# The add of 1e-9 under the softmax, on six columns written in pairs in place of four to four

## The chip, the cores and the metric

The kernel runs on one core of one Trainium2 chip. The metric is the device time of one execution in microseconds (us); of several runs the median is given. TensorE is called PE in the profile, VectorE DVE, ScalarE ACT, GpSimd POOL and SyncE SP; PEld is TensorE's loading of weights.

## The reference

Sliding-window attention with a distance bias, and behind it a feed-forward layer with a squared Relu, all in float32:

```python
# q, k, v: (8, 8, 576, 64): batch, heads, positions, head size
scores = scale * np.matmul(q, k.transpose(0, 1, 3, 2))
bias = slopes[:, None, None] * (-np.abs(rel))          # rel = query position - key position
mask = (rel >= 0) & (rel < 128)
scores = np.where(mask, scores + bias, -1e9)
scores = scores - np.max(scores, axis=-1, keepdims=True)
attn = np.exp(scores)
attn = attn / (np.sum(attn, axis=-1, keepdims=True) + 1e-09)
out = np.matmul(attn, v)
# heads side by side: x is (4608, 512); w_in (512, 2048), w_out (2048, 512)
h = np.maximum(x @ w_in, 0.0)
return h * h @ w_out
```

The change is at the 1e-09 and the division by the sum.

## The kernel before

The 4608 rows are cut into 9 chunks of 512, and each chunk has 4 pairs of heads. A *segment* is half a chunk for one pair of heads: 256 queries and two heads, as four blocks (`m` = 0 to 3) of 128 queries, two blocks to a head. There are 72 segments, and each runs through the same steps:

- *scores* on PE into PSUM;
- `top(m)`, four times on DVE: adds the distance table, writes the sums to the tile `t` (negated and scaled) and their minimum over the row, which is the negated maximum of the scores, to a column of the small tile `nm`;
- `exp(m)`, four times on ACT: the exponential with that column as bias, and the row's sum into another column of `nm`;
- `sums()`, on DVE: the add of 1e-9 to the four sums (L264) and the reciprocal (L265), both into a third group of columns of `nm`;
- `norm()`: the multiplication of `t` by the four factors, on POOL (L268, and L608 in the wide segments of the start), for segment 7 on DVE with one instruction for each block (L606);
- a transposition, the matmul with the values, and the split of the result `X` into a high and a low part `xu` (L307 and L310 in the start).

The feed-forward layer multiplies in float32 by splitting each operand into two parts and taking three matmuls of 128x512 for each tile. `gemm1` (L200) makes 128 rows of `h` from the four `xu` of a chunk; Relu (L210), square and the split into `hh` and `hl` (L219) follow; `gemm2` (L229) adds up the output over the 16 blocks of 128 rows. The weights arrive packed, 16 blocks of two DMAs (L165), and each block is converted in five steps: L171 (ACT), L173 and L175 (DVE), L177 (ACT, or POOL for blocks 0, 2 and 15), L179 (DVE).

The *start* covers the first chunk's attention in eight segments of their own kind (`Wide`: the scores of 128 queries against 256 keys, less where there are no earlier keys), the conversion of the weights, and the first chunk's feed-forward. Its transposes are done on PE (L615 for the own keys, L618 for the earlier ones) and copied out by ACT or DVE (L283, L622); L297 is the matmul with the values, L579 that of the scores, L127 matmuls on zeros that keep PE at work. A planner with fixed costs and due times decides the order of the steps on every engine of the start, and this order is kept: the costs that it uses are numbers in the code (0.4 us for `sums`) and do not change with the instructions. Each engine works off its list in order.

From the second chunk on, PE's order is written out by hand, with the attention of coming chunks between the matmuls of the feed-forward, and the scheduler of the framework orders the instructions of the other engines by a timeline of its own. There the norm's result is transposed in blocks on DVE (L319), goes through DRAM and back, and is masked on POOL (L332).

`nm` is one tile for each segment, from a pool of six. Its columns are: 0 to 3 the negated maxima, 4 to 7 the sums, 8 to 11 the sums plus 1e-9 and then their reciprocals. Both instructions of `sums` take four neighbouring float32 columns to four neighbouring ones.

Of the kernel before, what the change touches and what calls it, by code (L numbers as in the profile page):

```python
# [9 lines left out]
F32 = mybir.dt.float32  # L10
# [3 lines left out]
AF = mybir.ActivationFunctionType  # L14
ALU = mybir.AluOpType
# [46 lines left out]
class Kern:  # L62
# [68 lines left out]
    def room(self, c, p, name, shape, offset):  # L131
        if (c, p) != (0, NP - 1):
            return self.ld.tile(shape, F32, name=name)
        at = self.arena + (NF - 1) * 8192 + offset
        return self.nc.alloc_sbuf_tensor_at(f"{name}_", shape, F32, offset=at).ap()
# [103 lines left out]
class Segment:  # L239
# [9 lines left out]
    def top(self, m):  # L249
        self.nc.vector.tensor_tensor_reduce(  # L250
            self.t[:, m], self.t[:, m], self.K.nrel(2 * self.p + m // 2), -0.125, BIG,
            ALU.add, ALU.min, self.nm[:, m : m + 1],
        )

    def exp(self, m):
        nm = self.nm
        return self.nc.scalar.activation(  # L257
            self.t[:, m], self.t[:, m], AF.Exp, bias=nm[:, m : m + 1], scale=-1.0,
            accum_out=nm[:, 4 + m : 5 + m],
        )  # L260

    def sums(self):
        rec = self.nm[:, 8:12]
        self.nc.vector.tensor_scalar(rec, self.nm[:, 4:8], 1e-9, None, op0=ALU.add)  # L264
        self.nc.vector.reciprocal(rec, rec)  # L265

    def norm(self):
        self.nc.gpsimd.tensor_tensor(  # L268
            self.t, self.t, self.nm[:, 8:12].unsqueeze(2).to_broadcast([128, 4, 128]), op=ALU.mult
        )  # L270

    def turn(self):
# [98 lines left out]
class Couple:  # L371
# [113 lines left out]

    def room(self, s):
        K, G = self.K, self.both[s]
        G.t, G.nm = K.tp.tile([128, 4, 128], F32, name="t"), K.sm.tile([128, 12], F32, name="nm")

    def begin(self, s):  # L490
        self.room(s)
# [67 lines left out]
class Wide(Segment):  # L559
# [7 lines left out]
    def scores(self):  # L567
        K, nc, sg = self.K, self.nc, self.sg
        qk = K.qk[self.c, self.p]
        if self.k % 2:  # L570
            self.s = [b.rearrange("p (i c) -> p i c", i=2) for b in K.start_banks[0:2]]
        else:
            s = K.sc.tile([128, 4, 256], F32, name="s")
            self.s = [s[:, 0:2], s[:, 2:4]]
        for i in range(2):
            a, q0, k0 = self.first[i], 64 * (4 * sg + 2 * i) + (0 if sg == 0 else 640), 256 + 128 * (2 * sg + i)
            for j in range(2):
                r = slice(64 * j, 64 * j + 64)
                nc.tensor.matmul(  # L579
                    self.s[j][:, i, a:256], qk[r, q0 : q0 + 128], qk[r, k0 + a : k0 + 256], start=True, stop=True,  # L580
                    skip_group_check=True,
                )
        self.t = K.room_t[self.k % 4]
        self.nm = K.sm.tile([128, 12], F32, name="nm")

    def top(self, m):
        j, i = divmod(m, 2)
        a = self.first[i]
        self.nc.vector.tensor_tensor_reduce(
            self.t[:, m, a:256], self.s[j][:, i, a:256], self.K.wide[self.p][:, j, a:256], -0.125, BIG,  # L590
            ALU.add, ALU.min, self.nm[:, m : m + 1],
        )

    def exp(self, m):
        nm, t = self.nm, self.t[:, m, self.first[m % 2] : 256]
        self.nc.scalar.activation(
            t, t, AF.Exp, bias=nm[:, m : m + 1], scale=-1.0, accum_out=nm[:, 4 + m : 5 + m],
        )

    def norm(self):  # L600
        for i in (0, 1) if self.skip else (None,):
            m, a = (slice(None), 0) if i is None else (slice(i, 4, 2), self.first[i])
            t, rec = self.t[:, m, a:256], self.nm[:, 8:12][:, m]
            if self.k in NORMS:
                for j in range(t.shape[1]):
                    self.nc.vector.tensor_scalar(t[:, j], t[:, j], rec[:, j : j + 1], None, op0=ALU.mult)  # L606
                continue
            self.nc.gpsimd.tensor_tensor(t, t, rec.unsqueeze(2).to_broadcast(list(t.shape)), op=ALU.mult)  # L608

    def turn(self):  # L610
        self.place()
# [273 lines left out]
```

## Time and profile before

| | |
|---|---|
| median of 3 runs | 941.42 us (941.16 to 941.61) |
| profiled execution | 941.43 us, of which the span from first to last instruction is 939.7 us |
| PE busy | 930.5 us (99% of the span) |
| DVE, ACT, POOL busy | 501.4, 416.8, 210.6 us |
| granted clock of TensorE | 1.000 |
| L264, the add | 72 times, 139 ns at the least, 170 in the median, 1042 at the most |
| L265, the reciprocal | 72 times, 177, 178, 182 ns |

The page's own lines give, for each group of instructions, the line, the engine and operation, output <- input with shape and type, the count, the busy time, the mean of one, and the idle time of the engine just before them with what ended it. A row of the timeline gives start and duration in us; neighbouring instructions of the same kind stand in one row, with their count. PE's ends are modelled, since its matmuls overlap.

### The profile page before, as it was taken

Reading aid. Unit: us, or ns where it says so; the run is one execution under the profiler, and the core shown is the slowest. Engines: PE = TensorE matmul, PEld = TensorE weight load, DVE = VectorE, ACT = ScalarE, POOL = GpSimd, SP = SyncE. Lnnn points to the kernel's source line nnn. Section 1 sums busy time; section 2 is a strip of 40 time slices with the busy share of each in tenths; the row PEclk is TensorE's granted clock in tenths of the full one; section 3 lists DMA queues with packets and bytes.
Section 4 is the critical chain, followed back from the end, with each engine's and each line's share of the span. In section 5 each row is a group of like instructions: output and inputs, shape, how many; then the busy total and the mean of one; then the engine's idle time right before and its main releaser. Section 6 shows DMA issues by size and latency. Waiting matters only on the chain.

```text
span 939.7 us, 19487 instructions
## 1 busy us (share of the span) xinstructions
PE 930.5 (99%) x7488; PEld 783.0 (83%) x7492; DVE 501.4 (53%) x1334; ACT 416.8 (44%) x1107; POOL 210.6 (22%) x254
## 2 busy tenths in 40 slices
PE   9899999999999999999999999999999999999998
PEld 5688888888888888888888888888888888888886
DVE  6998874445554554545554444555455454433222
ACT  7898753343444444344433343344444444322222
POOL 4223331222222222222212222221222222220000
PEclk9999999999999999999999999999999999999999
DMA  9975423222432233232433232334322231111001
GB/s 345 404 282 167 134 74 116 73 71 85 129 86 84 76 99 112 67 85 76 128 85 84 69 110 83 85 85 115 101 75 85 74 94 42 39 46 45 1 0 45
DMA packets 72893, 95.26 MB, mean 101 GB/s; under 512 B 8032, under 2 KB 41952, under 8 KB 72800
## 3 DMA queue, kind: packets, MB, share of 16 engines
q1 hardware_dynamic: 72368, 93.36, 32.4%
q8 instruction: 59, 0.97, 0.4%
q10 hardware_dynamic: 432, 0.66, 0.2%
q14 instruction: 34, 0.28, 0.1%
HBM read 67.76 MB, written 26.21 MB: 100 GB/s over the span
## 4 chain that ended last, share of the span: by engine, by line
PE 94%; DMA 4%; ACT 1%; DVE 0%; issue 0%; SPq 0%; ACTq 0%; POOLq 0%
PE acc L229 43%; PE g L200 42%; PE s L539 5%; PE g L546 2%; DMA raw<-in_dram 2%; DMA cst<-in_dram 2%; PE s L546 1%; PE at L344 1%; DMA wide<-in_dram 1%; PE s L410 0%; PE at L410 0%; ACT t L468 0%; ACT raw L171 0%; DVE t L480 0%; ACT t L257 0%
## 5 line engine op out<-in xcount | busy, mean ns | idle before, releaser
L200 PE MATMUL g<-xu,w 128*128 128x512 f32 x1728 | 423.6, 394 | 1.3 <-issue 0.8
L200 PEld LDWEIGHTS g<-xu,w 128*128 128x128 f32 x1728 | 344.2, 209 | 57.1 <-issue 1.7
L229 PE MATMUL acc<-hh,w 128*128 128x512 f32 x1152 | 385.8, 396 | 0.0
L229 PEld LDWEIGHTS acc<-hh,w 128*128 128x128 f32 x1152 | 223.9, 194 | 46.0 <-issue 5.3
L210 ACT ACTIVATE r<-g 128x512 f32<-128x512 f32 x144 | 86.2, 598 | 352.5 <-PE g L200 352.4
L213 DVE TENSOR_TENSOR r<-r 128x512 f32<-128x512 f32 x129 | 93.1, 721 | 256.3 <-ACT r L210 256.3
L229 PE MATMUL acc<-hl,w 128*128 128x512 f32 x576 | 226.4, 393 | 0.0
L332 POOL TENSOR_SCALAR_AFFINE_SELECT pp<-pp 128x512 f32<-128x512 f32 x128 | 111.2, 869 | 219.4 <-DMA pp<-way 156.5
L219 DVE TENSOR_TENSOR hl<-r,hh 128x512 fp32r<-128x512 f32 x144 | 119.3, 829 | 74.8 <-ACT hh L217 72.7
L268 POOL TENSOR_TENSOR t<-t,nm 128x512 f32<-128x512 f32 x64 | 73.8, 1154 | 262.1 <-DVE nm L265 234.9
L229 PEld LDWEIGHTS acc<-hl,w 128*128 128x128 f32 x576 | 112.1, 195 | 19.8
L217 ACT CAST hh<-r 128x512 fp32r<-128x512 f32 x144 | 89.2, 619 | 78.6 <-DVE r L213 77.0
L257 ACT ACTIVATE t<-t,nm 128x128 f32<-128x128 f32 x256 | 100.0, 393 | 12.2 <-DVE nm L250 12.1
L319 DVE STREAM_TRANSPOSE pp<-t 128x512 f32<-128x512 f32 x64 | 45.1, 707 | 44.3 <-POOL t L268 37.6
L250 DVE CUSTOM_DVE_ANT_0 t<-t,cst 128x128 f32<-128x128 f32 x256 | 59.5, 295 | 1.0
L539 PE MATMUL s<-pp,v 64*64 64x128 f32 (+1 forms) x1792 | 52.0, 248 | 0.1
L539 PEld LDWEIGHTS s<-pp,v 64*64 64x64 f32 x1792 | 40.5, 134 | 10.2 <-issue 9.8
L257 ACT ACTIVATION_READ_ACCUMULATOR t<-t,nm 128x1 f32 x256 | 48.2, 188 | 0.0
L480 DVE COPY_PREDICATED t<-cst,s 64x256 f32<-64x256 int32 x100 | 44.6, 446 | 6.7 <-ACT t L461 3.6
L470 POOL MEMSET t<- 64x128 f32 (+1 forms) x44 | 10.0, 229 | 118.4 <-PE s L546 109.4
L527 ACT CAST xu<-s 128x512 fp32r<-128x512 f32 x28 | 16.4, 587 | 41.8 <-DVE t L480 26.8
L468 ACT COPY t<-g 64x256 f32<-64x256 f32 (+2 forms) x86 | 28.0, 340 | 3.8 <-PE g L546 1.0
(68 smaller groups left out, 483.2 us busy)
## 6 DMA issues: line engine op xcount, KB each, us to landing
raw<-in_dram SPq DMA_DIRECT2D x32, 512.0 KB, 8.7
way<-pp SPq DMA_DIRECT2D x256, 64.0 KB, 2.0
pp<-way SPq DMA_DIRECT2D x64, 256.0 KB, 2.7
qk<-in_dram SPq DMA_DIRECT2D x32, 320.0 KB, 3.1
v<-in_dram SPq DMA_DIRECT2D x32, 320.0 KB, 3.9
qk<-in_dram SPq DMA_DIRECT2D x38, 256.0 KB, 4.5
out_dram<-o SPq DMA_DIRECT2D x35, 256.0 KB, 2.7
v<-in_dram SPq DMA_DIRECT2D x3, 256.0 KB, 4.9
```

What stands on the lines that cost most here:

```text
L200: nc.tensor.matmul(g, w, xs[cc][:, part], start=i == 0, stop=i == 11)
L210: self.relu = nc.scalar.activation(r, g, AF.Relu)
L213: nc.vector.tensor_tensor(r, r, r, op=ALU.mult)
L217: nc.scalar.copy(hh, r)
L219: nc.vector.tensor_tensor(hl, r, hh.bitcast(F32), op=ALU.subtract)
L229: nc.tensor.matmul(self.acc[m], w, h, start=(f == 0 and i == 0), stop=(f == NF - 1 and i == 2))
L250: self.nc.vector.tensor_tensor_reduce(self.t[:, m], self.t[:, m], self.K.nrel(2 * self.p + m // 2), -0.125, BIG, ALU.add, ALU.min, self.nm ...
L257: return self.nc.scalar.activation(self.t[:, m], self.t[:, m], AF.Exp, bias=nm[:, m : m + 1], scale=-1.0, accum_out=nm[:, 4 + m : 5 + m],)
L268: self.nc.gpsimd.tensor_tensor(self.t, self.t, self.nm[:, 8:12].unsqueeze(2).to_broadcast([128, 4, 128]), op=ALU.mult)
L319: nc.vector.transpose(squares.rearrange("p b m c -> p m b c"), self.t.rearrange("p m (b c) -> p m b c", c=32))
L332: nc.gpsimd.affine_select(to, self.own, pattern=[[-32 * sign, 4], [0, 4], [-sign, 32]], compare_op=op, fill=0.0, base=0, channel_multiplie ...
L539: made.append(mm(to, w, x, start=first and n < 2, stop=not first, skip_group_check=True))
```

## The change

`nm` has 20 columns. The sums move to columns 0 to 3 and the maxima to 4 to 7. The add reads columns 0 to 5 as one row, the four sums and the first two maxima, and writes them in three pairs that begin at columns 8, 12 and 16. The reciprocal works in place on the first two pairs, so that the four factors lie in columns 8, 9, 12 and 13; the third pair is not used. The norms take the factors from there, as two heads by two blocks.

```diff
     def sums(self):
-        rec = self.nm[:, 8:12]
-        self.nc.vector.tensor_scalar(rec, self.nm[:, 4:8], 1e-9, None, op0=ALU.add)
-        self.nc.vector.reciprocal(rec, rec)
+        pairs = lambda a, n, step: self.nm[:, a : a + n * step].rearrange("p (n c) -> p n c", c=step)[:, :, 0:2]
+        self.nc.vector.tensor_scalar(pairs(8, 3, 4), pairs(0, 3, 2), 1e-9, None, op0=ALU.add)
+        self.nc.vector.reciprocal(pairs(8, 2, 4), pairs(8, 2, 4))
+        self.rec = pairs(8, 2, 4)

     def norm(self):
         self.nc.gpsimd.tensor_tensor(
-            self.t, self.t, self.nm[:, 8:12].unsqueeze(2).to_broadcast([128, 4, 128]), op=ALU.mult
+            *(x.rearrange("p (j i) c -> p j i c", j=2) for x in (self.t, self.t)),
+            self.rec.unsqueeze(3).to_broadcast([128, 2, 2, 128]), op=ALU.mult
         )
```

In `top` and `exp`, of both kinds of segment, the columns change to `nm[:, 4 + m : 5 + m]` for the maximum and `nm[:, m : m + 1]` for the sum. The norm of the wide segments follows:

```diff
-            m, a = (slice(None), 0) if i is None else (slice(i, 4, 2), self.first[i])
-            t, rec = self.t[:, m, a:256], self.nm[:, 8:12][:, m]
+            m, a = (slice(0, 2), 0) if i is None else (slice(i, i + 1), self.first[i])
+            t, rec = self.t.rearrange("p (j i) c -> p j i c", j=2)[:, :, m, a:256], self.rec[:, :, m]
             if self.k in NORMS:
-                for j in range(t.shape[1]):
-                    self.nc.vector.tensor_scalar(t[:, j], t[:, j], rec[:, j : j + 1], None, op0=ALU.mult)
+                for x in range(4):
+                    j, e = divmod(x, 2)
+                    self.nc.vector.tensor_scalar(t[:, j, e], t[:, j, e], rec[:, j, e : e + 1], None, op0=ALU.mult)
                 continue
-            self.nc.gpsimd.tensor_tensor(t, t, rec.unsqueeze(2).to_broadcast(list(t.shape)), op=ALU.mult)
+            self.nc.gpsimd.tensor_tensor(t, t, rec.unsqueeze(3).to_broadcast(list(t.shape)), op=ALU.mult)
```

More of the change, by code (lines that the diff above doesn't have):

```diff
@@ L251, in top @@
             self.t[:, m], self.t[:, m], self.K.nrel(2 * self.p + m // 2), -0.125, BIG,
-            ALU.add, ALU.min, self.nm[:, m : m + 1],
+            ALU.add, ALU.min, self.nm[:, 4 + m : 5 + m],
         )
@@ L257, in exp @@
         return self.nc.scalar.activation(
-            self.t[:, m], self.t[:, m], AF.Exp, bias=nm[:, m : m + 1], scale=-1.0,
-            accum_out=nm[:, 4 + m : 5 + m],
+            self.t[:, m], self.t[:, m], AF.Exp, bias=nm[:, 4 + m : 5 + m], scale=-1.0,
+            accum_out=nm[:, m : m + 1],
         )
     def sums(self):
-        rec = self.nm[:, 8:12]
-        self.nc.vector.tensor_scalar(rec, self.nm[:, 4:8], 1e-9, None, op0=ALU.add)
-        self.nc.vector.reciprocal(rec, rec)
+        pairs = lambda a, n, step: self.nm[:, a : a + n * step].rearrange("p (n c) -> p n c", c=step)[:, :, 0:2]
+        self.nc.vector.tensor_scalar(pairs(8, 3, 4), pairs(0, 3, 2), 1e-9, None, op0=ALU.add)
+        self.nc.vector.reciprocal(pairs(8, 2, 4), pairs(8, 2, 4))
+        self.rec = pairs(8, 2, 4)
     def norm(self):
         self.nc.gpsimd.tensor_tensor(
-            self.t, self.t, self.nm[:, 8:12].unsqueeze(2).to_broadcast([128, 4, 128]), op=ALU.mult
+            *(x.rearrange("p (j i) c -> p j i c", j=2) for x in (self.t, self.t)),
+            self.rec.unsqueeze(3).to_broadcast([128, 2, 2, 128]), op=ALU.mult
         )
@@ L487, in room @@
         K, G = self.K, self.both[s]
-        G.t, G.nm = K.tp.tile([128, 4, 128], F32, name="t"), K.sm.tile([128, 12], F32, name="nm")
+        G.t, G.nm = K.tp.tile([128, 4, 128], F32, name="t"), K.sm.tile([128, 20], F32, name="nm")
     def begin(self, s):
@@ L583, in scores @@
         self.t = K.room_t[self.k % 4]
-        self.nm = K.sm.tile([128, 12], F32, name="nm")
+        self.nm = K.sm.tile([128, 20], F32, name="nm")
     def top(self, m):
@@ L590, in top @@
             self.t[:, m, a:256], self.s[j][:, i, a:256], self.K.wide[self.p][:, j, a:256], -0.125, BIG,
-            ALU.add, ALU.min, self.nm[:, m : m + 1],
+            ALU.add, ALU.min, self.nm[:, 4 + m : 5 + m],
         )
@@ L596, in exp @@
         self.nc.scalar.activation(
-            t, t, AF.Exp, bias=nm[:, m : m + 1], scale=-1.0, accum_out=nm[:, 4 + m : 5 + m],
+            t, t, AF.Exp, bias=nm[:, 4 + m : 5 + m], scale=-1.0, accum_out=nm[:, m : m + 1],
         )
```

## The prediction

> **What bounds the kernel now.** I read the head of the page first, then the busy time of each engine in two stretches.
>
> ```profile
> span 939.7 us, 19487 instructions
> ## 1 busy us (share of the span) xinstructions
> PE 930.5 (99%) x7488; PEld 783.0 (83%) x7492; DVE 501.4 (53%) x1334; ACT 416.8 (44%) x1107; POOL 210.6 (22%) x254
> ```
>
> ```profile
> 0.00:48.00 48.00, 43.19 (x391) 28.85 (x396) 38.44 (x137) 37.35 (x109) 14.99 (x19) 1.00 0.99 375
> 48.00:939.70 891.70, 887.27 (x7098) 754.14 (x7097) 462.93 (x1198) 379.45 (x999) 195.64 (x235) 1.00 0.30 87
> ```
>
> The columns are the stretch, its length, then PE, PEld, DVE, ACT, POOL busy, granted clock, DMA share, GB/s. From 48 us on TensorE is busy 887.27 of 891.70 us and DVE only 462.93: there the add of 1e-9 cannot matter, except by making TensorE wait. What can move the end is how soon the dense stream of matmuls begins. So I read the start, in the groups of DVE work up to 52 us, then in time order.
>
> ```profile
> L264 DVE TENSOR_SCALAR nm<-nm 128x4 f32<-128x4 f32 x9 | 3.6, 405 | 0.2
> ...
> L622 DVE COPY pp<-acc 128x256 f32<-128x256 f32 x4 | 1.7, 414 | 0.2 <-PE acc L618 0.2
> ...
> L606 DVE TENSOR_SCALAR tw<-tw,nm 128x256 f32<-128x256 f32 x4 | 1.1, 350 | 0.0
> ```
>
> ```profile
> 27.55 0.68 DVE L622 COPY pp<-acc 128x512 f32<-128x512 f32 x1
> 28.15 1.21 DVE L175 SCALAR_TENSOR_TENSOR raw<-raw 128x1024 int32<-128x1024 int32 x1
> 29.28 0.41 DVE L310 TENSOR_TENSOR xu<-acc,xu 128x256 fp32r<-128x256 f32 x1
> 29.61 1.04 DVE L264 TENSOR_SCALAR nm<-nm 128x4 f32<-128x4 f32 x1
> 30.69 0.18 DVE L265 RECIPROCAL nm<-nm 128x4 f32<-128x4 f32 x1
> 30.91 1.14 DVE L606 TENSOR_SCALAR tw<-tw,nm 128x256 f32<-128x256 f32 x4
> 31.96 0.42 DVE L622 COPY pp<-acc 128x256 f32<-128x256 f32 x1
> 32.30 1.22 DVE L179 TENSOR_TENSOR w<-raw,w 128x1024 fp32r<-128x1024 f32 x1
> 33.43 0.42 DVE L310 TENSOR_TENSOR xu<-acc,xu 128x256 fp32r<-128x256 f32 x1
> ```
>
> An add of four columns has a mean of 405 ns in the start, and one of them takes 1.04 us in the middle of a stretch in which DVE has no idle time. What it waited for shows in POOL's rows of the same time, beside the add one pair earlier:
>
> ```profile
> 24.12 0.62 DVE L264 TENSOR_SCALAR nm<-nm 128x4 f32<-128x4 f32 x1
> ```
>
> ```profile
> 22.82 1.90 POOL L608 TENSOR_TENSOR tw<-tw,nm 128x1024 f32<-128x1024 f32 x1 [1.37 <-DVE nm L265]
> 25.12 1.61 POOL L608 TENSOR_TENSOR tw<-tw,nm 128x256 f32<-128x256 f32 x2 [0.41 <-DVE nm L265]
> 29.48 1.15 POOL L177 CAST w<-raw 128x1024 fp32r<-128x1024 f32 x1 [2.75 <-ACT tw L596]
> ```
>
> The add at 24.12 ends at 24.74, POOL's norm at 24.72. The add at 29.61 ends at 30.65, POOL's cast at 30.63. Both adds end where POOL ends: they start and are then held until POOL is through. Not every DVE instruction is held so:
>
> ```profile
> 73.30 0.18 DVE L265 RECIPROCAL nm<-nm 128x4 f32<-128x4 f32 x1
> ```
>
> ```profile
> 73.22 0.73 POOL L332 TENSOR_SCALAR_AFFINE_SELECT pp<-pp 128x512 f32<-128x512 f32 x1 [8.53 <-DMA pp<-way]
> ```
>
> Here a reciprocal of the same four columns runs its ordinary 0.18 us in the middle of a POOL instruction.
>
> **The change part by part.** *The add.* 72 adds stay 72, with six columns in place of four, two of them wasted. Whether the new form is held as the old one is shown by no row. One end is that it is: 1.04 us again. The other is the free duration. I get that from the rows before: nine adds take 3.6 us, of which two are 1.04 and 0.62; an add behind nothing I take at 0.17 us, as its neighbour of equal size, the reciprocal, takes 0.18. I take 0.17, since the reciprocal is the nearest one-input row on the same tile and is not held. Two more columns cost nothing I can see: L622 takes 414 ns for 256 columns, under 2 ns a column.
>
> [...]
>
> *The reciprocal* now reads and writes two pairs; four columns still, 0.18 us, 0 either way. *Top and exp* swap their columns only: 0. The add now also reads two maxima, which DVE itself wrote well before the exponentials it waits for anyway: 0. *The larger tile*, 20 columns for 12: 0. *The norm* on POOL reads its factors in two levels in place of one:
>
> ```profile
> L608 POOL TENSOR_TENSOR tw<-tw,nm 128x1024 f32<-128x1024 f32 x3 | 5.7, 1896 | 1.8 <-DVE nm L265 1.4 <-ACT tw L596 0.4
> L608 POOL TENSOR_TENSOR tw<-tw,nm 128x512 f32<-128x512 f32 x4 | 4.2, 1042 | 0.0
> ```
>
> 1024 elements in four rows take 1896 ns, 512 in two 1042: 1.67 ns an element and some 0.19 us fixed, with no sign of a price for a row. I take 0; the bound is in the rivals.
>
> *What the path gets.* First term, the adds before 27.5 us. The one at 24.12 alone gives DVE 0.62 - 0.17 = 0.45 us. But the copy L622 at 27.55 reads what TensorE transposes:
>
> ```profile
> 26.10 0.60 PE L615 MATMUL at<-cst,tw 128*128 128x128 f32 x4
> 26.53 0.60 PE L618 MATMUL acc<-cst,tw 128*128 128x128 f32 x4
> ```
>
> L618 ends at 27.13, and with a hand-over of 0.05 us (the reciprocal at 30.69 starts 0.04 after the add ends) the copy cannot start before 27.18. TensorE runs its own list without a gap there, so it does not come earlier: at most 27.55 - 27.18 = 0.37 us is kept, whatever the earlier adds give. I take 0.37; the lower end is 0.
>
> Second term, the add at 29.61. The cast on POOL waits for L175 (28.15), so both move by 0.37: cast 29.11 to 30.26, add at 29.24. Free, add and reciprocal are through by some 29.65. Behind them L606, the norm of segment 7 on DVE, is queued, a TENSOR_SCALAR from SBUF to SBUF as the add was. Its 256 columns take 350 ns where L622 needs 414 for as many, so it runs in a faster mode, and I take it to be held as the old add was: it starts when POOL ends, at 30.26 + 0.04 = 30.30, not 30.91. Together 0.61 us, of which 0.24 is this term. Were L606 not held, it would start at 29.68 and 1.2 us would be won.
>
> [...]
>
> Then the path to the dense stream:
>
> ```profile
> 41.98 2.37 DVE L179 TENSOR_TENSOR w<-raw,w 128x1024 fp32r<-128x1024 f32 x2
> ```
>
> ```profile
> 43.45 3.04 PE g L200 x12
> 46.49 0.79 issue
> 47.29 3.06 PE g L200 x12
> 50.35 2.80 PE acc L229 x12
> 53.15 2.80 PE g L200 x12
> ```
>
> ```profile
> 50.17 1.22 DVE L179 TENSOR_TENSOR w<-raw,w 128x1024 fp32r<-128x1024 f32 x1
> ```
>
> L179 at 41.98 (two in a row, the first over by about 43.2) completes the second block of weights, and its matmuls start at 43.45: DVE's delay passes to TensorE. The next group at 47.29 follows the relu of the one before, then the stream is dense. All of this moves by 0.6. Later covers: the next block's L179 ends at 51.39, its matmuls start at 53.15, so TensorE can come 1.7 us earlier before DVE is late there.
>
> Sum: the profiled execution took 941.43 us, 1.7 of it outside the span, 0.01 over the median of 941.42. 941.43 - 0.37 - 0.24 = 940.8 us. The lower end is 940.0: L606 free (1.2 us) and the spread of the runs, 0.25 us below. The upper is 941.8: nothing won, and runs up to 0.4 us higher. A ceiling for any gain: nine adds at 3.6 us less nine at 0.17 leave 2.1 us.
>
> **The rivals.** *L606 is not held.* The whole wait goes: 941.43 - 1.2 = 940.2. For it speaks that nothing shows L606 held, against it its 350 ns. 0.15.
>
> [...] 0.2.
>
> *Slower: the norm takes longer.* If POOL pays for the second level of the factors, the norm at 22.82 ends after 24.72; TensorE turns its result at 26.10. It is late once the norm is 1.38 us longer, 73% of its 1.90. At double the price TensorE is 0.52 late, L622 at 27.55 moves back by that in place of forward by 0.37, and only the second term remains: 941.43 + 0.52 - 0.24 = 941.7. To be 1.9 us slower it would need 1.9 + 0.24 + 1.38 = 3.5 us more per norm. Against it the two L608 rows. 0.05.
>
> **How the numbers follow.** Main case 0.55, L606 free 0.15, nothing 0.2, norm 0.05, and 0.05 for an order of the later instructions that the planner may choose otherwise and that makes TensorE wait, of either sign. 0.2% is 1.9 us, about what a measurement of this kernel can tell from no change. The ceiling of 2.1 us lies barely above it, so faster has 0.02; slower 0.03 for the norm and the order; the rest, 0.95, is within. The range 940.0 to 941.8 holds the first three cases.
>
> **What would show it.** The adds of the start at some 0.17 us, none ending with a POOL row; L606 starting within 0.1 us of the end of POOL's cast (right) or well inside it (the first rival); the reciprocal still at 0.18; norms at 1042 and 1896 ns; the matmuls now at 47.29 starting near 46.7, and as many us later in the span as now. Wrong would be an add that still ends with POOL, a reciprocal that does, or a gap on TensorE after 48 us that is not there now.

## The result and the profile after

The changed kernel takes 949.66 us (median of 5 runs, 949.45 to 949.92) against 941.47 us of the kernel before beside it (5 runs, 941.16 to 941.61). The ratio is 1.0088, with a 95% interval of 1.0076 to 1.0099: 8.2 us slower, far outside the predicted range. The head of the page and the two stretches again, for the kernel after (columns as before):

```profile
span 947.9 us, 19491 instructions
PE 939.5 (99%) x7492; PEld 786.6 (83%) x7492; DVE 498.1 (53%) x1334; ACT 416.8 (44%) x1107; POOL 214.1 (23%) x254
```

```profile
0.00:48.00 48.00, 43.96 (x400) 29.49 (x401) 38.16 (x138) 38.64 (x110) 14.96 (x19) 1.00 0.99 375
48.00:939.70 891.70, 891.06 (x7076) 753.67 (x7075) 458.56 (x1195) 377.01 (x996) 199.12 (x235) 1.00 0.29 85
```

There is no new gap: TensorE is busy 891.06 of 891.70 us, 3.8 us more than before, and yet that stretch holds fewer matmuls (7076 for 7098 recorded). The granted clock is 1.00 in both. DVE's busy time fell. So the time went into the matmuls themselves. The chain of waits in the middle of the run, before and then after (start, duration, what):

```profile
399.07 2.76 PE acc L229 x12
401.83 2.76 PE g L200 x12
404.60 2.76 PE acc L229 x12
```

```profile
398.26 2.80 PE g L200 x12
401.06 2.80 PE acc L229 x12
403.86 2.80 PE g L200 x12
```

In this stretch a group of twelve matmuls of 128x512 takes 2.80 us in place of 2.76. In the groups of the page, before and then after, each mean is 2 ns longer:

```profile
L200 PE MATMUL g<-xu,w 128*128 128x512 f32 x1728 | 423.6, 394 | 1.3 <-issue 0.8 <-DVE xu L528 0.6
L229 PE MATMUL acc<-hh,w 128*128 128x512 f32 x1152 | 385.8, 396 | 0.0
```

```profile
L200 PE MATMUL g<-xu,w 128*128 128x512 f32 x1728 | 428.4, 396 | 1.3 <-issue 0.8 <-DVE xu L530 0.5
L229 PE MATMUL acc<-hh,w 128*128 128x512 f32 x1152 | 388.5, 398 | 0.0
```

The starts of the single matmuls show two rhythms. Around 402 us they follow each other in 229 and 231 ns in turn before, a mean of 230.0, and in 232, 233 and 235 ns after, a mean of 233.3; twelve make 2.760 and 2.800 us. (In the kernel before some groups are at 2.79 or 2.80 too.) Over the groups that can be timed from their first matmul to the next group's (109 of gemm1, 137 of gemm2) the mean goes from 2.775 to 2.806 and from 2.795 to 2.828; with 144 groups of each kind that is 144 x (0.031 + 0.033) = 9.2 us. The stretch from the second gemm1 group (47.29 before, 46.15 after) to the end grew by 9.3 us, 892.4 to 901.7. What the start won comes off: 9.3 - 1.1 = 8.2 us.

The start itself went much as predicted. DVE after, then POOL, then TensorE:

```profile
26.82 0.69 DVE L625 COPY pp<-acc 128x512 f32<-128x512 f32 x1
27.43 1.21 DVE L175 SCALAR_TENSOR_TENSOR raw<-raw 128x1024 int32<-128x1024 int32 x1
28.57 0.42 DVE L312 TENSOR_TENSOR xu<-acc,xu 128x256 fp32r<-128x256 f32 x1
28.90 0.15 DVE L264 TENSOR_SCALAR nm<-nm 128x6 f32<-128x6 f32 x1
29.08 0.18 DVE L265 RECIPROCAL nm<-nm 128x4 f32<-128x4 f32 x1
29.30 1.60 DVE L609 TENSOR_SCALAR tw<-tw,nm 128x256 f32<-128x256 f32 x4
30.82 0.41 DVE L625 COPY pp<-acc 128x256 f32<-128x256 f32 x1
```

```profile
28.77 1.19 POOL L177 CAST w<-raw 128x1024 fp32r<-128x1024 f32 x1 [3.17 <-ACT tw L598]
```

```profile
26.19 0.60 PE L621 MATMUL acc<-cst,tw 128*128 128x128 f32 x4
```

(L625, L312 and L609 are L622, L310 and L606 of before, L621 is L618.) The add lies inside POOL's cast and takes 0.15 us; over the whole run the 72 adds have a mean of 157 ns, and none is over 163. The norm of segment 7 behind it takes the wait: four instructions in 1.60 us, for 1.14 before.

### The profile page after: what moved, and what is told of

It reads as the page before. It is cut to its first block, busy times and chain, and to the rows that moved or that the text cites. A ratio compares the mean times of both kernels' runs of the same rounds, so it can differ in the third digit from the quotient of the medians.

```text
span 947.9 us, 19491 instructions
## 1 busy us (share of the span) xinstructions
PE 939.5 (99%) x7492; PEld 786.6 (83%) x7492; DVE 498.1 (53%) x1334; ACT 416.8 (44%) x1107; POOL 214.1 (23%) x254
## 4 chain that ended last, share of the span: by engine, by line
PE 95%; DMA 4%; DVE 1%; ACT 1%; issue 0%; SPq 0%; POOLq 0%
PE acc L229 43%; PE g L200 42%; PE s L541 5%; PE g L548 2%; DMA raw<-in_dram 2%; PE s L548 1%; DMA wide<-in_dram 1%; PE at L346 1%; DMA qk<-in_dram 1%; ACT t L470 0%; PE s L412 0%; PE at L412 0%; DVE t L482 0%; ACT t L257 0%; DVE t L486 0%
## 5 line engine op out<-in xcount | busy, mean ns | idle before, releaser
L200 PE MATMUL g<-xu,w 128*128 128x512 f32 x1728 | 428.4, 396 | 1.3 <-issue 0.8
L200 PEld LDWEIGHTS g<-xu,w 128*128 128x128 f32 x1728 | 346.0, 210 | 59.7 <-issue 1.7
L269 POOL TENSOR_TENSOR t<-t,nm 128x512 f32<-128x512 f32 x64 | 76.0, 1189 | 262.1 <-DVE nm L265 232.6
```

Of the source, the lines that this page charges most:

```text
L200: nc.tensor.matmul(g, w, xs[cc][:, part], start=i == 0, stop=i == 11)
L269: self.nc.gpsimd.tensor_tensor(*(x.rearrange("p (j i) c -> p j i c", j=2) for x in (self.t, self.t)), self.rec.unsqueeze(3).to_broadcast([ ...
```

## Why the place of a tile became the theory

Between the two kernels no matmul of the feed-forward differs. What differs for it is where its operands lie: a slot of `nm` takes 96 bytes a partition in place of 64 in the compiled program, there are six, and `xu`, `r`, `hh`, `hl` and `o` are laid out behind them, so all of these begin 192 bytes further on. The weights, ahead of `nm`, stay. Theory, *place*: the operands that the matmuls stream (`xu` in gemm1, `hh` and `hl` in gemm2) lie worse. Rival, *timing*: the earlier start or the new instructions leave TensorE in the slower rhythm. Below, "moved by" is against the kernel before.

## The experiments

**Place alone, and instructions alone.** In e1 the kernel before gets the larger tile and nothing else:

```diff
-K.sm.tile([128, 12], F32, name="nm")
+K.sm.tile([128, 20], F32, name="nm")
```

> The kernel before with nm at 20 columns; no instruction differs, but xu, r, hh, hl and o lie 192 bytes further on in SBUF, as in the changed kernel. Address theory (the matmuls run at 2.80 us a group of 12 in place of 2.76 because the operands that they stream lie elsewhere): 949.7 us or, with the start of before, up to 951, groups at 2.80. Timing theory (the new instructions, or the stream starting 1.1 us earlier, leave TensorE in the slower rhythm): 941.4 us, groups at 2.76.

950.42 us, ratio 1.0098 (1.0082 to 1.0113), with these groups:

```profile
398.84 2.80 PE g L200 x12
401.64 2.80 PE acc L229 x12
404.44 2.80 PE g L200 x12
```

The instructions of before, with their operands 192 bytes on, have the whole loss. In e2 the changed kernel keeps its add, but has the room of before (16 columns take 64 bytes):

```diff
-pairs(8, 3, 4), pairs(0, 3, 2)      # and nm of 20 columns
+pairs(7, 3, 3), pairs(0, 3, 2)      # and nm of 16 columns
```

> The changed kernel with the three written pairs three columns apart (7, 10, 13) and nm at 16 columns, so that everything behind it lies where it lay before; the add still reads six columns in one row and writes three pairs. Address theory: the 1.1 us won in the start is kept and the groups go back to 2.76: 940.3 us. Timing theory: 949.7 us, groups at 2.80.

940.64 us, ratio 0.9992 (0.9982 to 1.0001), with these groups:

```profile
398.06 2.76 PE acc L229 x12
400.81 2.76 PE g L200 x12
```

The loss is gone with the new instructions in place. The timing theory fell with these two. In e3 the changed kernel gets 64 bytes more, 256 in all:

```diff
+self.sm.tile([128, 16], F32, name="fill", bufs=1)
```

> The changed kernel with an unused tile of 64 bytes behind nm: xu, r, hh, hl, o lie 256 bytes further on than before, in place of 192. Address theory: another value than 949.7 is possible, and if what counts repeats every 256 bytes, 940.3. Timing theory: 949.7, as the instructions and their times are those of the changed kernel.

940.68 us, ratio 0.9993 (0.9983 to 1.0003): with still more room taken the loss is gone. It is the place, not the room taken. (This filler, and those of e5, e8, e11 and e12, is the first tile of its pool and so lies ahead of `nm`, not behind it as the expectations say; `nm` moves too, but no matmul reads it.)

**Which operand.** In e4 the kernel before gets an unused tile of 192 bytes ahead of `r`; `xu` stays.

```diff
+self.hp.tile([128, 48], F32, name="fill", bufs=1)
```

> The kernel before with an unused tile of 192 bytes ahead of r: r, hh, hl and o lie 192 bytes further on, xu and nm where they were. Address theory: if the operands of the second matmul (hh, hl) are what counts, about 950 us, if those of the first (xu) do, 941.4, if both, between. Timing theory: 941.4.

950.15 us, ratio 1.0094 (1.0079 to 1.0109): the whole loss, though only the operands of gemm2 moved. Up to 134 us six groups of gemm1 still run at 230.0 ns a matmul, beside gemm2 at 233.3; from 138 us on gemm1 too is at 2.79 to 2.82 us a group, though its own operand had not moved:

```profile
398.72 2.79 PE g L201 x12
401.52 2.80 PE acc L230 x12
404.32 2.81 PE g L201 x12
```

In e5 it is the other way round, `xu` by 192 and the rest by 256:

```diff
+self.sm.tile([128, 48], F32, name="fill", bufs=1)
+self.hp.tile([128, 16], F32, name="fill", bufs=1)
```

> The kernel before with unused tiles that move xu by 192 bytes and r, hh, hl and o by 256 (a move that left the changed kernel fast). Theory A, each matmul's rhythm depends on where its own moving operand lies: gemm1 (reads xu) at 2.80 us a group, gemm2 (reads hh, hl) at 2.76, time some 945 to 946 us. Theory B, only hh and hl count and gemm1 takes the rhythm over from the group before: 941.4. Theory C, any such operand at +192 holds the whole stream in the slow rhythm: about 950.

948.28 us, ratio 1.0074 (1.0059 to 1.0089), above what theory A gave and below C.

```profile
397.64 2.80 PE g L202 x12
400.44 2.76 PE acc L231 x12
403.20 2.80 PE g L202 x12
406.00 2.76 PE acc L231 x12
```

Here gemm1 is slow and gemm2 fast, in turn, as theory A has it. But this holds for only about half of the groups of gemm2, those right behind the attention's matmuls left out. The others, among them all from 673 us on, run at 232.8 to 234.8 ns; of the same groups the kernel before has none that is slow after 260 us. So an operand at +192 was slow in every group that can be timed, and one at its old place can be either; beside a slow neighbour, as here and in e4, it is often slow. What sets that is not settled. In e6 only `hl` (and `o`) move by 192:

```diff
         hh = self.hp.tile([128, 512], F32R, name="hh")
+        if (c, f) == (0, 0):
+            self.hp.tile([128, 48], F32, name="fill1", bufs=1)
         hl = self.hp.tile([128, 512], F32R, name="hl")
```

> The kernel before with an unused tile of 192 bytes between hh and hl: only hl (a third of gemm2's matmuls read it) and o move by 192. Theories B and C, one such operand is enough to hold the stream in the slow rhythm: about 950 us. If hh is what counts, or each matmul stands by itself: 941.4, or at most a third of gemm2's share more, 943.

942.44 us, ratio 1.0011 (1.0001 to 1.0021): one operand in three costs little, and does not hold the stream in the slow rhythm.

```profile
398.91 2.77 PE acc L231 x12
401.68 2.76 PE g L200 x12
```

The matmuls of such a gemm2 group follow each other in 231.1 ns on average, which is what two at 230.0 and one at 233.3 give. Theory B fell with e5, where `xu` alone at +192 made gemm1 slow, and theory C falls here. Theory A holds for the moved operands; the unmoved ones that are slow in e4 and e5 it does not explain.

**Place, or distance to the weights.** In e7 192 unused bytes are put ahead of everything, so that weights and moving operands shift together:

```diff
+self.nc.alloc_sbuf_tensor("fill", [128, 48], F32)
 self.nc.alloc_sbuf_tensor("arena", [128, NF * 2048], F32)
```

> The kernel before with 192 unused bytes ahead of all its data in SBUF: weights, xu, hh, hl and everything else move by 192 together. If the place of the moving operands by itself counts: about 950 us, 2.80 a group. If their place against the weights' counts: 941.4, 2.76 a group.

941.15 us, ratio 0.9999 (0.9990 to 1.0009). `xu`, `hh` and `hl` lie at exactly the bytes at which e1 took 950.42 us:

```profile
399.04 2.76 PE acc L230 x12
401.80 2.76 PE g L201 x12
404.56 2.76 PE acc L230 x12
```

This I had not expected: what counts is the distance, not the place. e8 takes a distance of +64, with an unused tile ahead of `nm`:

```diff
+self.sm.tile([128, 16], F32, name="fill", bufs=1)
```

> The kernel before with an unused tile of 64 bytes behind nm: xu, r, hh, hl and o move by 64. If every move that is not a multiple of 256 bytes is slow: about 950 us. If 192 is a particular place: 941.4. Timing theory (its place in SBUF does nothing): 941.4, which the two slow runs of before's instructions already speak against.

948.42 us, ratio 1.0075 (1.0060 to 1.0090). e13 makes the same distance from the other side, the weights by 192 and all behind them by 256:

```diff
+self.nc.alloc_sbuf_tensor("fill0", [128, 48], F32)
 self.nc.alloc_sbuf_tensor("arena", [128, NF * 2048], F32)
 self.arena = self.nc.sbuf_base - NF * 8192
+self.nc.alloc_sbuf_tensor("fill1", [128, 16], F32)
```

> The kernel before with 192 unused bytes ahead of the weights and 64 more behind them: the weights move by 192, the operands that move past them (xu, hh, hl) and all behind by 256, so their distance grows by 64. If the place of the moving operands by itself counts: they lie a whole 256 bytes on, as in a kernel that was fast, and the time is 941.4. If their distance to the weights counts: about 948.4 us, the time of the kernel with 64 bytes more.

947.95 us, ratio 1.0072 (1.0055 to 1.0089), the price of e8 within the intervals.

```profile
398.33 2.78 PE g L202 x12
401.12 2.79 PE acc L231 x12
403.90 2.79 PE g L202 x12
```

The single matmuls repeat e8's own pattern too (in a gemm1 group around 404 us 230, 226 or 227, 231, 229, 230, 232, 235 ns in both). The operands are a whole 256 bytes on, where e3 was fast; only their distance to the weights is e8's. Place by itself is out.

**More distances.** e11 and e12 are e8 with tiles of 128 and 32 bytes.

```diff
+self.sm.tile([128, 32], F32, name="fill", bufs=1)      # e11
+self.sm.tile([128, 8], F32, name="fill", bufs=1)       # e12
```

> The kernel before with an unused tile of 128 bytes behind nm: xu, r, hh, hl and o move by 128 against the weights. If what counts repeats every 128 bytes: 941.4. If only every 256 bytes: between 948 and 951, like 64 and 192.

> The kernel before with an unused tile of 32 bytes behind nm: xu, r, hh, hl and o move by 32 against the weights. If any distance but the one of before (and whole 256 bytes more) is slow: 947 to 951. If a move of 32 stays within what counts as one place: 941.4.

e11 takes 950.63 us, ratio 1.0101 (1.0087 to 1.0115), e12 940.69 us, 0.9996 (0.9987 to 1.0005). Together, for all moving operands against the weights:

| moved by | kernel | us | ratio |
|---|---|---|---|
| 0 | before, beside the runs | 941.1 to 941.5 | 1 |
| 32 | e12 | 940.69 | 0.9996 |
| 64 | e8, e13 | 948.42, 947.95 | 1.0075, 1.0072 |
| 128 | e11 | 950.63 | 1.0101 |
| 192 | e1, after | 950.42, 949.66 | 1.0098, 1.0088 |
| 256 | e3 (with the new add) | 940.68 | 0.9993 |

The distance in the kernel before is 160 bytes more than a multiple of 256, for `xu`, `hh` and `hl` alike. That it repeats every 256 bytes rests on the one point at 256.

**What the change itself is worth.** e9 is e2 again, over more runs; e10 is e2 with the add on two pairs read and two written, four columns:

```diff
-pairs(7, 3, 3), pairs(0, 3, 2)
+pairs(7, 2, 3), pairs(0, 2, 2)
```

> The changed kernel with nm at 16 columns again, against the kernel before, for a narrower interval. If the terms of the start were right (0.61 us, or the 0.8 us of the first look) and nothing else differs: a ratio of 0.9990 to 0.9995, 940.3 to 940.8 us.

> The same kernel, but the add reads two pairs and writes two pairs (four columns), in place of six in one row to three pairs; the places in SBUF are those of before, the norms read their factors as in the changed kernel. If the form of the add is what frees it from POOL: adds of the start up to 1.04 us again, ending with a POOL row, and 941.4 us. If it is the layout of nm that frees it: adds of 0.15 us and 940.6.

e9 takes 940.40 us, ratio 0.9993 (0.9984 to 1.0002), e10 941.31 us, 1.0002 (0.9994 to 1.0011). In e10 the hold is back, on the layout of e9:

```profile
29.34 1.09 DVE L264 TENSOR_SCALAR nm<-nm 128x4 f32<-128x4 f32 x1
```

```profile
29.21 1.18 POOL L177 CAST w<-raw 128x1024 fp32r<-128x1024 f32 x1 [2.75 <-ACT tw L598]
```

The add ends at 30.43, the cast at 30.39. In e2, the kernel of e9, the add lies inside the cast (28.75 to 29.90) and is free:

```profile
28.88 0.15 DVE L264 TENSOR_SCALAR nm<-nm 128x6 f32<-128x6 f32 x1
```

So it is the form that frees the add: beside the same cast, six columns in one row to three pairs took 0.15 us in e2, two pairs to two pairs 1.09 us in e10. The version with 16 columns has the lowest median here, 0.9 us under e10 on the same chip, where the slowest run of e9 (940.67) lies below the fastest of e10 (940.91); against the kernel before, its interval still reaches 1.

## Why the prediction was wrong

**The step that failed** is the sentence "*The larger tile*, 20 columns for 12: 0". I read it as a cost on the instructions that touch the tile, and they do cost nothing. It moved the operands of the matmuls by 192 bytes against their weights, and that costs some 9 us: e1 has it alone (+9.0), e2 lacks it alone (-0.8). With it fell the premise that "what can move the end is how soon the dense stream of matmuls begins": I took the rate of that stream as fixed, and it went from 230.0 to 233.3 ns a matmul. No rival held it. The single case for slower was a longer norm, and the chance of 0.03 came from the norm and the planner's order.

**The sign that I named for being wrong** failed too. I would have looked for a gap on TensorE after 48 us; there is none. A matmul that streams more slowly shows as busy time, 887.27 to 891.06 us, and was to be read from the duration of equal groups.

**What could have been seen.** In the profile before, the groups at 50.35 and 53.15 take 2.80 us and most later ones 2.76, at the same granted clock of 1.00. I quoted the two rows and did not ask why the same twelve matmuls have two durations. That is a rate which can change, over 288 groups, and 0.04 us on each would be 11.5 us. Which way a shift would turn it, no row of before could tell.

**The terms of the start** were right in kind and nearly in size. To read them, the moment of the loads must be taken out. The scores that begin at 8.80 before begin at 8.45 after:

```profile
8.80 0.93 PE L579 MATMUL s<-qk 64*128 64x128 f32 x8
```

```profile
8.45 0.93 PE L581 MATMUL s<-qk 64*128 64x128 f32 x8
```

This differs from kernel to kernel with the instructions of before as well (8.26 in e1, 8.42 in e12, 8.68 in e7), so it is no work of the change; 0.35 of the 1.14 us by which the stream starts earlier is of this kind. From those scores to the wide copy it is 18.75 us before (27.55 - 8.80), 18.75 in e1 and 18.74 in e12, and 18.37 after (26.82 - 8.45), 18.37 in e2 and 18.38 in e9: the first term is 0.38 us, predicted 0.37. The cap held as well. L621 ends at 26.79 and the copy starts at 26.82.

The second term: from the scores to the second copy it is 23.16 us before and 22.37 after, 0.79 in all, which leaves 0.41 for it against 0.24. The 0.24 rested on two estimates of mine that no row of before showed: that the add would be free in its new form, and that the norm of segment 7, by its 350 ns against 414, would be held in its place. No run shows a faster mode, and none a term of 0.24. What the run after shows is the add at 0.15 us inside the cast and the first of the four instructions of the norm at 0.82: the hold did move to the norm, and the rival in which it runs free is out. What I missed is that the held instruction starts at 29.30, and ends 0.16 us after the cast (0.82 us, for 0.34 of each of the other three), where I let it start 0.04 us after the cast's end and run its full 0.35. That is 0.23 us; the cast, which starts 0.02 later behind the wide copy and is 0.04 longer than before, takes 0.06 back, and 0.17 is left. My sign for this term was wrong as well: by its start, well inside the cast, the row would have spoken for the rival; its duration shows the hold. The sum by measured terms is 0.8 us; e2 and e9 measured 0.8 and 0.7 us less than the kernel before beside them (941.40 and 941.06), each with an interval that reaches 1. *Norm* and *reciprocal* were 0: the norms of the start still take 1896 and 1042 ns, the reciprocals 0.18 us.

That nothing changes, which had 0.2, is out for the start, since the add is free there at 0.15 us; "norm slower" has no sign, by the norms just given.

## What to carry to other kernels

A change to the size of a small tile moves everything that is allocated behind it, here by 192 bytes, and in e1 that alone cost 9.0 us. Where a dense stream of matmuls bounds the kernel, compare the addresses of its operands and of its weights before and after, and the duration of equal groups, before reading anything else; and when a change of a few instructions costs a per cent spread evenly over the run, try it with a filler that puts the rest back. Give a scratch tile a size that keeps its padded slot, or put it behind the operands that matter.

## What the runs showed of the hardware

- A matmul of 128x512 in this stream, with a weight load for each (1728 of both in gemm1, L200), follows the one before in 230.0 or 233.3 ns on average, at a granted clock of 1.00. Which of the two depends on the distance in SBUF between its moving operand and the weights: around 400 us the groups took 2.75 to 2.77 us at the distance of before, +32 and +256 bytes (e7, e12, e3), 2.80 at +128 and +192 (e11, e1), and +64 lies between, 2.78 to 2.79 in e13, some 232.5 ns. That it is the distance and not the place, e7 shows against e1 (941.15 and 950.42 us, operands at the same bytes) and e13 against e3 (947.95 and 940.68 us).
- Why the distance matters, by 1.4% of a matmul (230.0 to 233.3 ns), is open. In the dense stretches of e13 the weights are the only part moved by 192 that TensorE reads; but no run had the loads of the weights without the streaming of the operand, and whether the one delays the other no run shows.
- The distance does not settle the rhythm alone. At the distance of before the stream is at 233.3 in some stretches up to 260 us and at 230.0 after, but for one group of gemm1 in four (233.2 on average, its last matmuls at 230.0). In e4 gemm1 changes from one to the other at 138 us without a change of its operands. What switches it is open.
- A DVE instruction that is held by POOL shows as a longer one from its own start (the add 1.04 us before, for 0.17 in the median, and 1.09 in e10; the norm's first instruction 0.82 after, for 0.34), and ended 0.02 to 0.04 us (the add, before and in e10) or 0.16 us (256 columns, after) behind POOL.
